# Splitting the first load by partitions and moving W2 from the end to the start of a decode kernel

## The chip, the core and the metric

The kernel runs on one core of one Trainium2 chip. The metric is device time in microseconds (us), the median of several executions. The engines are TensorE (PE in the profile, with its weight loads as PEld), VectorE (DVE), ScalarE (ACT), GpSimd (POOL) and SyncE (SP). SyncE does no arithmetic here: it issues the large loads. The data is moved by sixteen DMA engines.

## What is computed

One decode step of attention over a long cache, beside a small dense branch, mixed by a gate. Two sequences (B = 2), one token each, model width 448, 16 query heads and 8 key/value heads of width 256, and 32,768 cached positions.

```python
g = sigmoid((x * gate_w).sum(-1, keepdims=True))
# first branch (A): attention over the cache
q = (x @ wq).reshape(B, 1, 16, 256)            # wq: 448 x 4096
p = softmax(q @ k_cache.T * 256 ** -0.5)       # each K/V head serves two query heads
a = (p @ v_cache).reshape(B, 1, 4096) @ wo     # wo: 4096 x 448
# second branch (B): dense, GELU, dense
b = gelu(x @ w1 + b1) @ w2 + b2                # w1: 448 x 1792, w2: 1792 x 448
out = g * a + (1 - g) * b
```

The K and V caches are 2 x 8 x 32,768 x 256 bf16 values each, 268 MB each. They are nearly all of the bytes that are read.

## The kernel before: the parts that matter here

The caches come in as tiles of 128 partitions x 64 KB (8 MB). There are 32 K tiles and 32 V tiles. They rotate through a ring of three slots. SyncE walks through a fixed order of loads, and before each load it waits until PE is done with what lay in the slot.

```python
WOP = (0, 16, 28, 31, 32)          # WO is loaded and used in four pieces of these chunks
DQ = Dm // 2                       # 224: the output row is made in two column tiles
...
order = [("WQ", 0), ("W1", 0)]
for i in range(NTILES + LAG):      # K tiles, and V tiles two behind
    ...
order += [("V", LASTV), ("W2", 0), ("WO", 0)]
...
def released(d):                   # what PE must have done before a slot is filled again
    return {"K": ("S", idx, NCK // 2 - 1), "V": ("PV", idx), "WQ": "QT", "W1": "HT"}[kind]
```

The issue of the loads, on SyncE (cut to the kinds that matter):

```python
if kind == "WQ":      # 384 rows as 128 partitions x 24,576 B, and the 64 rows that are left
    parts = [(wq_f, A_wq[0:KC * P, :].rearrange("(p k) n -> p (k n)", p=P), "d_wq0"),
             (wq_r, A_wq[KC * P:Dm, :].rearrange("p (h n) -> (p h) n", h=2), "d_wq1")]
    for i, (o, src, _) in enumerate(parts):
        dma(lambda e, o=o, src=src: e.dma_start(o, src), "slot0", ("wq", i))
...
elif kind == "W2":
    dma(lambda e: e.dma_start(w2_f, B_w2.rearrange("(p f) n -> p (f n)", p=P)), "d_w2", "w2")
elif kind == "WO":
    for i in range(len(WOP) - 1):
        ...
```

The order on PE: the query projection (QT), the gate (GG), the first dense layer (HT) and the bias of the second (B2); then the loop over tiles (S: scores of a K tile; PV: probabilities times a V tile; OT: the sum of a group); and at the end the transposed attention vector (TT), the second dense layer (FB) and the output projection (FIN).

```python
do_QT(); do_GG(); do_HT(); do_B2()
...                                   # the loop over tiles
PV(LASTV - 1); PV(LASTV)
E.wait("pool", "ts1")
OT(NG - 1)
TT()
do_FB()
E.wait("dve", "at")
for i in range(len(WOP) - 1):
    FIN(i)
...
def do_FB():                          # line 459
    E.wait("dve", "hT")
    E.wait_total("d_w2")
    for fc in range(FC):              # 14 chunks
        for q in range(2):            # two column tiles of 224
            E.ins(lambda e, fc=fc, q=q: e.matmul(
                ps_a[64 * q:64 * q + Bn, :], hT_bf[:, fc, :], w2_v[:, fc, q * DQ:(q + 1) * DQ], ...))

def FIN(i):                           # line 551
    E.wait(f"pW{i}", ("wo", i))
    for c in range(WOP[i], WOP[i + 1]):
        for q in range(2):
            E.ins(lambda e, c=c, q=q: e.matmul(
                ps_a[64 * q:64 * q + Bn, :], attnT[:, c:Bn * NC:NC],
                wo_v[:, c * Dm + q * DQ:c * Dm + (q + 1) * DQ], ...))
```

When FIN is done, VectorE copies the first 224 columns of the output and ScalarE the others, and SyncE stores the row. Each copy raises one shared semaphore ("mix"), on which SyncE waits once.

Of the kernel before, what the change touches and what calls it, by code (L numbers as in the profile page):

```python
# [125 lines left out]
def bass_gated_mix__gqa_block_cached__dense_activation_gelu__decode_kernel(  # L126
# [26 lines left out]
    Bn, Sq, Dm = A_x.shape  # L153
    _, Hkv, Sk, Dh = A_k_cache.shape
    HD = A_wq.shape[1]
    Hq = HD // Dh
    Fd = B_w1.shape[1]
    assert Sq == 1 and Dh == 256 and Hq == 2 * Hkv and Bn == 2
    P = 128
    R = 128  # L160
    CR = 16
    NCK = R // CR
# [8 lines left out]
    KC = 3  # L171
    KR = Dm - KC * P
    assert 2 * KR == P
    HW, HF = HD // 2, Fd // 2
    FC = Fd // P
    SLOT = R * Dh
# [3 lines left out]
    assert (NTILES - LAG) % UNIT == 0  # L180
    PIECES = (64, 32, 32)
    NC = HD // P
    WOP = (0, 16, 28, 31, 32)
    DQ = Dm // 2
    GELU_C = 0.7978845608028654
    GELU_A = 0.044715

    sch = _Sched()
    for nm in ("pe", "act", "dve", "pool", "sp"):
        sch.stream(nm, 1)  # L190
    sch.stream("mix", 1)
    for i in range(NB):
        sch.stream(f"slot{i}", 16)
    for i in range(len(PIECES)):
        sch.stream(f"pV{i}", 16)
    for i in range(len(WOP) - 1):
        sch.stream(f"pW{i}", 16)
    for nm in ("d_w1", "d_w2", "d_x", "d_gw", "d_b", "d_out"):
        sch.stream(nm, 16)

    with contextlib.ExitStack() as es:
# [14 lines left out]
        b2_f = gp_sb  # L216
# [6 lines left out]
        dg = sb("dg", [Bn, Bn], dt.float32)  # L223
# [6 lines left out]
        hT_bf = sb("hT_bf", [P, FC, Bn], dt.bfloat16)  # L230
# [4 lines left out]
        out_sb = pexp[0:Bn, 0:Dm]  # L235
# [33 lines left out]
            b, kvh = grp(g)  # L269
            return cache[b, kvh, t * P * R:(t + 1) * P * R, :].rearrange("(p r) d -> p (r d)", p=P)  # L270

        W_WQ, W_W1 = KC * HD + HW, KC * Fd + HF
        assert W_WQ + W_W1 <= SLOT and (NC + FC) * Dm <= SLOT
        LASTV = NTILES - 1
        order = [("WQ", 0), ("W1", 0)]
        for i in range(NTILES + LAG):
            if i < NTILES:
                order.append(("K", i))
            if i >= LAG and i - LAG < LASTV:
                order.append(("V", i - LAG))  # L280
        order += [("V", LASTV), ("W2", 0), ("WO", 0)]
        slot_of = {("WQ", 0): 0, ("W1", 0): 0}
        rot = [d for d in order if d[0] in "KV" and d != ("V", LASTV)]
        for n, d in enumerate(rot):
            slot_of[d] = (n + 1) % NB
        s_wo = slot_of[("V", LASTV - 2)]
        slot_of[("WO", 0)] = slot_of[("W2", 0)] = s_wo
        slot_of[("V", LASTV)] = slot_of[("K", NTILES - 1)]
        assert len({s_wo, slot_of[("V", LASTV)], slot_of[("V", LASTV - 1)]}) == NB
        before_of, fill_no, occ, uses = {}, {}, {}, [0] * NB  # L290
        for d in order:
            s = slot_of[d]
            if d in (("W1", 0), ("WO", 0)):
                before_of[d] = []
                occ[s] = occ[s] + [d]
                continue
            before_of[d] = occ.get(s, [])
            occ[s] = [d]
            if d[0] in "KV" and d != ("V", LASTV):
                uses[s] += 1  # L300
                fill_no[d] = uses[s]

        def released(d):
            kind, idx = d
            return {"K": ("S", idx, NCK // 2 - 1), "V": ("PV", idx), "WQ": "QT", "W1": "HT"}[kind]

        cut = lambda s, lo, n: ring[:, s * SLOT + lo:s * SLOT + lo + n]
        wq_f, wq_r = cut(0, 0, KC * HD), cut(0, KC * HD, HW)
        wq_v = wq_f.rearrange("p (k n) -> p k n", k=KC)
        w1_f, w1_r = cut(0, W_WQ, KC * Fd), cut(0, W_WQ + KC * Fd, HF)  # L310
        w1_v = w1_f.rearrange("p (k n) -> p k n", k=KC)
        w2_f = cut(s_wo, NC * Dm, FC * Dm)
        w2_v = w2_f.rearrange("p (f n) -> p f n", f=FC)
        wo_v = cut(s_wo, 0, NC * Dm)

# [43 lines left out]
        def prog_sp(E):  # L359
            def dma(fn, stream, key):  # L360
                E.ins(fn, key=key, stream=stream)

            for d in order:
                for pd in before_of[d]:
                    E.wait("pe", released(pd))
                kind, idx = d
                if kind == "WQ":
                    parts = [(wq_f, A_wq[0:KC * P, :].rearrange("(p k) n -> p (k n)", p=P), "d_wq0"),
                             (wq_r, A_wq[KC * P:Dm, :].rearrange("p (h n) -> (p h) n", h=2), "d_wq1")]
                    for i, (o, src, _) in enumerate(parts):  # L370
                        dma(lambda e, o=o, src=src: e.dma_start(o, src), "slot0", ("wq", i))
                elif kind == "W1":
                    parts = [(w1_f, B_w1[0:KC * P, :].rearrange("(p k) n -> p (k n)", p=P)),
                             (w1_r, B_w1[KC * P:Dm, :].rearrange("p (h n) -> (p h) n", h=2))]
                    for i, (o, src) in enumerate(parts):
                        dma(lambda e, o=o, src=src: e.dma_start(o, src), "d_w1", ("w1", i))  # L376
                elif kind == "W2":
                    dma(lambda e: e.dma_start(w2_f, B_w2.rearrange("(p f) n -> p (f n)", p=P)), "d_w2", "w2")
                elif kind == "WO":
                    src = A_wo.rearrange("(p c) n -> p (c n)", p=P)  # L380
                    for i in range(len(WOP) - 1):
                        c0, c1 = WOP[i] * Dm, WOP[i + 1] * Dm
                        dma(lambda e, src=src, c0=c0, c1=c1: e.dma_start(wo_v[:, c0:c1], src[:, c0:c1]), f"pW{i}", ("wo", i))
                elif d == ("V", LASTV):
                    src, base, r0 = kv_src(A_v_cache, idx), slot_of[d] * SLOT, 0
                    for i, n in enumerate(PIECES):
                        c0, c1 = r0 * Dh, (r0 + n) * Dh
                        dma(lambda e, c0=c0, c1=c1: e.dma_start(ring[:, base + c0:base + c1], src[:, c0:c1]),
                            f"pV{i}", ("piece", i))
                        r0 += n  # L390
                else:
                    src = kv_src(A_k_cache if kind == "K" else A_v_cache, idx)
                    dma(lambda e, src=src, d=d: e.dma_start(cut(slot_of[d], 0, SLOT), src),
                        f"slot{slot_of[d]}", ("fill", d))
            E.wait_total("mix")
            dma(lambda e: e.dma_start(out[:, 0, :], out_sb), "d_out", "out")
            E.wait_total("d_out")

        def prog_pe(E):
# [4 lines left out]
            def do_QT():  # L404
# [3 lines left out]
                    E.ins(lambda e, k=k, src=src: e.matmul(ps_x[:, k, :], src, ident_b[0:Bn, 0:Bn],  # L408
                                                           start=True, stop=True), key=("XT" if k == KC + 1 else None))
                E.wait("act", "xT")  # L410
                E.wait("slot0", ("wq", 1))
                for h in range(Hq):
                    kvh, hh = h // 2, h % 2
                    for j in range(2):
# [17 lines left out]
                            key=("QR" if (s == NS - 1 and Q == 3) else None))  # L432

            def do_HT():
                E.wait_total("d_w1")
                E.wait("dve", "omB")
                for fc in range(FC):
                    for kc in range(KC):
                        E.ins(lambda e, fc=fc, kc=kc: e.matmul(
                            ps_hT[:, fc, :], w1_v[:, kc, fc:Fd:FC], xT[:, kc, :],  # L440
                            start=(fc == 0 and kc == 0), stop=False, skip_group_check=True))
                    for hf in range(2):
                        E.ins(lambda e, fc=fc, hf=hf: e.matmul(
                            ps_hT[hf * 64:hf * 64 + 64, fc, :], w1_r[:, fc:HF:FC], xT[:, KC + hf, :],
                            start=False, stop=True, skip_group_check=True),
                            key=("HT" if (fc == FC - 1 and hf == 1) else None))

            def do_B2():
                E.wait("dve", "b2f")
                for q in range(2):  # L450
                    E.ins(lambda e, q=q: e.matmul(ps_a[64 * q:64 * q + Bn, :], dg[:, :], b2_f[:, q * DQ:(q + 1) * DQ],
                                                  start=False, stop=False, skip_group_check=True))

            def do_FB():
                E.wait("dve", "hT")
                E.wait_total("d_w2")
                for fc in range(FC):
                    for q in range(2):
                        E.ins(lambda e, fc=fc, q=q: e.matmul(
                            ps_a[64 * q:64 * q + Bn, :], hT_bf[:, fc, :], w2_v[:, fc, q * DQ:(q + 1) * DQ],  # L460
                            start=False, stop=False, skip_group_check=True))

            def do_GG():
                E.wait("pool", "A0")
# [82 lines left out]
            def FIN(i):  # L547
                E.wait(f"pW{i}", ("wo", i))
                for c in range(WOP[i], WOP[i + 1]):
                    for q in range(2):  # L550
                        E.ins(lambda e, c=c, q=q: e.matmul(  # L551
                            ps_a[64 * q:64 * q + Bn, :], attnT[:, c:Bn * NC:NC],
                            wo_v[:, c * Dm + q * DQ:c * Dm + (q + 1) * DQ], start=False, stop=(c == NC - 1),
                            skip_group_check=True), key=("FIN" if (c == NC - 1 and q == 1) else None))

            def TT():
                E.wait("dve", "on")
                for b in range(Bn):
                    for dh in range(8):
# [6 lines left out]
            do_QT()  # L566
            do_GG()
            do_HT()
            do_B2()
            def K(idx):  # L570
                S(idx)
                if idx % NT == NT - 1:
# [14 lines left out]
            E.loop((NTILES - LAG) // UNIT, steps, ("dve", ("PT", 0)))  # L587
            PV(LASTV - 1)
            PV(LASTV)
            E.wait("pool", "ts1")  # L590
            OT(NG - 1)
            TT()
            do_FB()
            E.wait("dve", "at")
            for i in range(len(WOP) - 1):
                FIN(i)
# [1 line left out]
        def prog_act(E):  # L598
# [54 lines left out]
            E.loop(NG - 2, step, ("dve", ("PT", 0)))  # L653
            chain(NG - 1)
            E.wait("pe", "FIN")
            E.ins(lambda e: e.copy(out_sb[:, DQ:Dm], ps_a[64:64 + Bn, :]), key="mixa", stream="mix")

        def prog_dve(E):
            E.ins(lambda e: e.memset(ps_o[:, :], 0.0), key="o0")
# [130 lines left out]
            E.wait("pe", "TT")  # L790
            E.ins(lambda e: e.tensor_copy(attnT[:, :], ps_aT), key="at")
            E.wait("pe", "FIN")
            E.ins(lambda e: e.tensor_copy(out_sb[:, 0:DQ], ps_a[0:Bn, :]), key="mixd", stream="mix")

        progs = {"pool": prog_pool, "sp": prog_sp, "pe": prog_pe, "act": prog_act, "dve": prog_dve}
        engs = {nm: _Eng(sch, nm) for nm in progs}
# [45 lines left out]
```

## Time and profile before

| | |
|---|---|
| device time, median of 3 | 1273.89 us (1273.33 to 1274.27) |
| span of the profiled execution | 1271.6 us |
| mean granted TensorE clock | 0.783 |
| first load issued | 0.74 us after the span's start |
| first transpose of K0 on VectorE | 36.44 us |
| last WO matmuls (line 551) | 1267.90 to 1269.60 us |
| store of the output issued | 1270.05 us |

The profile is one execution of the program. It has the busy time of each engine, a digit per fortieth of the span for how busy each was, the DMA queues, the chain of work that ended last, groups of equal instructions, and the issues of transfers with the time until they landed. A line such as `L551` is a line of the kernel. In the timeline, a row gives the start, the length, the engine, the line, the operation, what is written and read, the count, and in brackets how long the engine stood idle before it and what ended that. The trace also holds the record of every DMA packet and the completion event of each of the sixteen DMA engines for each transfer.

### The profile page before, as it was taken

The numbers are of one execution on the slowest core, as the hardware profiler recorded it, in microseconds if no ns is written. First come the engines' busy times: TensorE is split into PE (matmuls) and PEld (weight loads), VectorE is DVE, ScalarE is ACT, GpSimd is POOL, SyncE is SP. The second block draws the span as 40 slices with busy tenths as digits, with TensorE's granted clock in tenths as the row PEclk, the third lists the DMA queues.
The fourth block names the chain that finished last, engine by engine and source line by source line (L and its number), as shares of the span: only waits on it lengthen the run. The fifth ranks groups of instructions, "written<-read, shape, count | busy, mean of one in ns | idle before, by whom it ended". The sixth has DMA issues, their size and how long they took to land.

```text
span 1271.6 us, 8088 instructions
## 1 busy us (share of the span) xinstructions
PE 698.9 (55%) x4544; PEld 146.0 (11%) x2016; DVE 685.8 (54%) x528; ACT 43.7 (3%) x183; POOL 3.3 (0%) x14
## 2 busy tenths in 40 slices
PE   4566566644466443665544665455664437655465
PEld 3111011100011100111100111000110001111012
DVE  2875537655365563556735466453755636566341
ACT  1000000000000000000000000000000000000000
POOL 1000000000000000000000000000000000000000
PEclk9988788767887777887778887778876778877686
DMA  9999999999999999999999999999999999999998
GB/s 404 441 434 431 429 429 435 431 439 434 431 429 435 437 431 437 435 431 429 433 439 431 437 435 429 431 433 439 431 437 433 431 431 433 439 431 433 437 423 359
DMA packets 10971, 547.59 MB, mean 431 GB/s; under 512 B 1352, under 2 KB 1616, under 8 KB 1872
## 3 DMA queue, kind: packets, MB, share of 16 engines
q1 hardware_dynamic: 10804, 547.43, 99.6%
q8 instruction: 8, 0.13, 0.0%
q10 hardware_dynamic: 156, 0.01, 0.0%
q14 instruction: 3, 0.02, 0.0%
HBM read 547.43 MB, written 0.00 MB: 431 GB/s over the span
## 4 chain that ended last, share of the span: by engine, by line
DMA 63%; DVE 21%; PE 13%; issue 3%; SPq 0%; another core or an unknown queue 0%
DMA ring<-in_A_k_cache_dram 60%; DVE ring L722 19%; PE ps_o L335 4%; PE ps_s L490 3%; PE ps_s L335 3%; DMA ring<-in_A_wo_dram 3%; DVE mx L726 1%; PE ps_o L539 1%; PE ps_m L499 0%; PE ps_m L504 0%; DVE gmax L728 0%; DVE gmx L732 0%; PE ps_f L551 0%; SPq L376 0%
## 5 line engine op out<-in xcount | busy, mean ns | idle before, releaser
L722 DVE STREAM_TRANSPOSE ring<-ring 128x2048 uint32<-128x2048 uint32 x256 | 565.2, 2275 | 390.2 <-DMA ring<-in_A_k_cache_dram 389.9
L490 PE MATMUL ps_s<-ring,Abd 128*128 128x512 bf16 x1024 | 427.0, 417 | 428.7 <-DVE ring L722 428.3
L335 PE MATMUL ps_s<-ring,Abd 128*128 128x512 bf16 x1024 | 423.3, 413 | 0.0
L490 PEld LDWEIGHTS ps_s<-ring,Abd 128*128 128x128 bf16 x1024 | 106.1, 104 | 852.0 <-DVE ring L722 480.1
L335 PE MATMUL ps_o<-ring,PT 128*24 128x512 bf16 x1504 | 112.9, 408 | 0.0
L539 PE MATMUL ps_o<-ring,PT 128*24 128x512 bf16 x544 | 58.1, 427 | 12.6 <-DMA ring<-in_A_v_cache_dram 12.6
L509 PE MATMUL ps_f<-o_sb,selg 128*32 128x257 f32 x32 | 17.0, 634 | 83.5 <-DVE o_sb L763 83.5
L763 DVE SCALAR_TENSOR_TENSOR o_sb<-ps_o,mask,o_sb 128x256 f32<-128x256 f32 x112 | 54.1, 483 | 8.9 <-PE ps_o L539 5.0
L726 DVE TENSOR_REDUCE mx<-ps_s 128x1 f32<-128x1024 f32 x16 | 19.6, 1224 | 59.9 <-PE ps_s L335 59.9
L636 ACT ACTIVATE negm<-ps_m 128x1 f32<-128x1 f32 x16 | 2.7, 171 | 1156.4 <-PE ps_m L504 1156.4
L739 DVE STREAM_TRANSPOSE PT<-pexp 128x1024 bf16<-128x1024 bf16 x16 | 19.9, 1245 | 36.8 <-PE ps_o L335 36.8
L539 PEld LDWEIGHTS ps_o<-ring,PT 128*24 128x24 bf16 x544 | 14.7, 100 | 104.1 <-issue 86.9
L736 DVE COPY ls<-lsum 128x1 f32<-128x1 f32 x16 | 2.5, 154 | 31.8 <-ACT pexp L640 31.8
L630 ACT COPY Abd<-qrep 32x16 bf16 (+1 forms) x128 | 19.4, 199 | 0.6
L640 ACT ACTIVATE pexp<-ps_s,negm 128x1024 bf16<-128x1024 f32 x16 | 17.8, 1113 | 1.7
L499 PE MATMUL ps_m<-ident_f,mx 128*1 128x128 f32 x32 | 6.1, 271 | 21.1 <-DVE mx L726 21.1
L760 DVE TENSOR_SCALAR o_sb<-ps_o,mask 128x256 f32<-128x256 f32 x16 | 7.6, 475 | 17.7 <-PE ps_o L335 17.7
L509 PEld LDWEIGHTS ps_f<-o_sb,selg 128*32 128x32 f32 x32 | 2.9, 139 | 101.6 <-DVE o_sb L763 99.5
L504 PE MATMUL ps_m<-ones_f,gmx 1*128 1x1 f32 x32 | 6.0, 256 | 9.9 <-DVE gmx L732 9.9
L728 DVE TENSOR_REDUCE gmax<-ps_m 1x2 f32<-1x128 f32 x16 | 4.5, 279 | 7.5 <-PE ps_m L499 7.5
L420 PE MATMUL ps_s<-xT,ring 128*128 128x2 bf16 x128 | 3.6, 165 | 8.1 <-DMA ring<-in_A_wq_dram 8.1
L504 PEld LDWEIGHTS ps_m<-ones_f,gmx 1*128 1x128 f32 x32 | 4.7, 183 | 14.6 <-DVE gmx L732 14.6
(76 smaller groups left out, 64.1 us busy)
## 6 DMA issues: line engine op xcount, KB each, us to landing
ring<-in_A_v_cache_dram SPq DMA_DIRECT2D x1, 4096.0 KB, 27.0
ring<-in_A_v_cache_dram SPq DMA_DIRECT2D x2, 2048.0 KB, 33.7
ring<-in_A_wq_dram SPq DMA_DIRECT2D x1, 3072.0 KB, 10.5
ring<-in_A_wo_dram SPq DMA_DIRECT2D x1, 1792.0 KB, 38.2
ring<-in_B_w_dram SPq DMA_DIRECT2D x1, 1568.0 KB, 34.3
ring<-in_B_w_dram SPq DMA_DIRECT2D x1, 1344.0 KB, 13.6
ring<-in_A_wo_dram SPq DMA_DIRECT2D x1, 1344.0 KB, 41.0
ring<-in_A_wq_dram SPq DMA_DIRECT2D x1, 512.0 KB, 11.3
```

Source lines behind the costliest of these rows:

```text
L335: return e.add_instruction(mybir.InstMatmult(name=f"I-{nc.next_id()}", engine=mybir.EngineType.PE, ldweights=False, ins=[e.lower_ap(x), e. ...
L490: fn = lambda e, o=o, x=x, st=st, sp=sp, s=s, w=w: e.matmul(o, a_win(s, w), x, start=st, stop=sp, skip_group_check=True)
L504: E.ins(lambda e: e.matmul(ps_m[:, C_BC:C_BC + 1], gmx[:, :], ones_f[0:1, 0:1], start=True, stop=True), key=("M2", g))
L509: E.ins(lambda e: e.matmul(ps_oa, selg[:, :], o_sb[:, :], start=False, stop=False, skip_group_check=True), key=("OT", g))
L539: fn = lambda e, o=o, x=x, wt=wt, st=st, sp=sp, j=j: e.matmul(o, wt, x, start=st, stop=sp, skip_group_check=True)
L630: E.ins(lambda e, o=o, Q=Q, c=c: e.copy(o[:, :, c:c + 2], qrep[32 * Q:32 * Q + 32, :, bass.ds(E.dyn(2 * g, 2), 2)]), key=(("A", g) if (Q = ...
L640: E.ins(lambda e: e.activation(pexp[:, :].rearrange("p (r i a) -> p i r a", r=CR, i=2), ps_s[:, :].rearrange("p (i r a) -> p i r a", i=2, ...
L722: E.ins(lambda e: e.transpose(k_words(idx, blk), k_words(idx, blk)), key=("T", idx, blk))
L726: E.ins(lambda e: e.tensor_reduce(mx[:, :], ps_s[:, :], AX.X, ALU.max), key=("MX", g))
L739: E.ins(lambda e: e.transpose(PT[:, :], pexp[:, :]), key=("PT", g))
L760: E.ins(lambda e, p=p, m=m: e.tensor_scalar(o_sb[:, 0:Dh], p, m, None, op0=ALU.mult), key=("OS0", g))
L763: E.ins(lambda e, p=p, m=m: e.scalar_tensor_tensor(out=o_sb[:, 0:Dh], in0=p, scalar=m, in1=o_sb[:, 0:Dh], op0=ALU.mult, op1=ALU.add), key= ...
```

## The change

Three things change together. The first load, the 128 partitions of wq, is issued as two transfers: partitions 0 to 15, and then partitions 16 to 127. W2 is loaded right behind W1 at the start, in the same slot, and the second dense layer (FB) is done there, so that the end of the kernel has only the attention output and WO left. The output row is made in four column tiles of 112 columns in place of two of 224, so that each engine copies two of them at the end. The pieces of WO have 14, 12, 4 and 2 chunks, in place of 16, 12, 3 and 1. The purpose is to take work and a transfer from the end of the kernel, and to let the first load begin in a small step.

```diff
-    WOP = (0, 16, 28, 31, 32)
-    DQ = Dm // 2
+    WOP = (0, 14, 26, 30, 32)
+    DQ = Dm // 4
...
-        order = [("WQ", 0), ("W1", 0)]
+        order = [("WQ", 0), ("W12", 0)]
...
-        order += [("V", LASTV), ("W2", 0), ("WO", 0)]
+        order += [("V", LASTV), ("WO", 0)]
...
-            return {"K": ("S", idx, NCK // 2 - 1), "V": ("PV", idx), "WQ": "QT", "W1": "HT"}[kind]
+            return {"K": ("S", idx, NCK // 2 - 1), "V": ("PV", idx), "WQ": "QT", "W12": "FB"}[kind]
...
-                    parts = [(wq_f, A_wq[0:KC * P, :].rearrange("(p k) n -> p (k n)", p=P), "d_wq0"),
-                             (wq_r, A_wq[KC * P:Dm, :].rearrange("p (h n) -> (p h) n", h=2), "d_wq1")]
+                    src = A_wq[0:KC * P, :].rearrange("(p k) n -> p (k n)", p=P)
+                    parts = [(wq_f[0:16, :], src[0:16, :]), (wq_f[16:P, :], src[16:P, :]),
+                             (wq_r, A_wq[KC * P:Dm, :].rearrange("p (h n) -> (p h) n", h=2))]
...
-                elif kind == "W1":
+                elif kind == "W12":
                     parts = [(w1_f, B_w1[0:KC * P, :].rearrange("(p k) n -> p (k n)", p=P)),
-                             (w1_r, B_w1[KC * P:Dm, :].rearrange("p (h n) -> (p h) n", h=2))]
+                             (w1_r, B_w1[KC * P:Dm, :].rearrange("p (h n) -> (p h) n", h=2)),
+                             (w2_f, B_w2.rearrange("(p f) n -> p (f n)", p=P))]
...
-            E.wait_total("mix")
+            E.wait("dve", "mix")
+            E.wait("act", "mix")
...
             def do_HT():
-                E.wait_total("d_w1")
+                E.wait_total("d_w12")
...
-            def do_B2():
+            def do_FB():
                 E.wait("dve", "b2f")
-                for q in range(2):
+                for q in range(4):
...
-            def do_FB():
                 E.wait("dve", "hT")
-                E.wait_total("d_w2")
                 for fc in range(FC):
-                    for q in range(2):
+                    for q in range(4):
...
             do_HT()
-            do_B2()
+            do_FB()
...
             OT(NG - 1)
             TT()
-            do_FB()
             E.wait("dve", "at")
...
-            E.ins(lambda e: e.copy(out_sb[:, DQ:Dm], ps_a[64:64 + Bn, :]), key="mixa", stream="mix")
+            for q in (2, 3):
+                E.ins(lambda e, q=q: e.copy(out_sb[:, q * DQ:(q + 1) * DQ], ps_a[32 * q:32 * q + Bn, :]),
+                      key=("mix" if q == 3 else None))
...
-            E.ins(lambda e: e.tensor_copy(out_sb[:, 0:DQ], ps_a[0:Bn, :]), key="mixd", stream="mix")
+            for q in (0, 1):
+                E.ins(lambda e, q=q: e.tensor_copy(out_sb[:, q * DQ:(q + 1) * DQ], ps_a[32 * q:32 * q + Bn, :]),
+                      key=("mix" if q == 1 else None))
```

More of the change, by code (lines that the diff above doesn't have):

```diff
@@ L190, in bass_gated_mix__gqa_block_cached__dense_activation_gelu__decode_kernel @@
         sch.stream(nm, 1)
-    sch.stream("mix", 1)
     for i in range(NB):
@@ L197, in bass_gated_mix__gqa_block_cached__dense_activation_gelu__decode_kernel @@
         sch.stream(f"pW{i}", 16)
-    for nm in ("d_w1", "d_w2", "d_x", "d_gw", "d_b", "d_out"):
+    for nm in ("d_w12", "d_x", "d_gw", "d_b", "d_out"):
         sch.stream(nm, 16)
@@ L270, in kv_src @@
             return cache[b, kvh, t * P * R:(t + 1) * P * R, :].rearrange("(p r) d -> p (r d)", p=P)
-        W_WQ, W_W1 = KC * HD + HW, KC * Fd + HF
-        assert W_WQ + W_W1 <= SLOT and (NC + FC) * Dm <= SLOT
+        W_WQ, W_W12 = KC * HD + HW, KC * Fd + HF + FC * Dm
+        assert W_WQ + W_W12 <= SLOT
         LASTV = NTILES - 1
-        order = [("WQ", 0), ("W1", 0)]
+        order = [("WQ", 0), ("W12", 0)]
         for i in range(NTILES + LAG):
@@ L280, in bass_gated_mix__gqa_block_cached__dense_activation_gelu__decode_kernel @@
                 order.append(("V", i - LAG))
-        order += [("V", LASTV), ("W2", 0), ("WO", 0)]
-        slot_of = {("WQ", 0): 0, ("W1", 0): 0}
+        order += [("V", LASTV), ("WO", 0)]
+        slot_of = {("WQ", 0): 0, ("W12", 0): 0}
         rot = [d for d in order if d[0] in "KV" and d != ("V", LASTV)]
@@ L286, in bass_gated_mix__gqa_block_cached__dense_activation_gelu__decode_kernel @@
         s_wo = slot_of[("V", LASTV - 2)]
-        slot_of[("WO", 0)] = slot_of[("W2", 0)] = s_wo
+        slot_of[("WO", 0)] = s_wo
         slot_of[("V", LASTV)] = slot_of[("K", NTILES - 1)]
@@ L292, in bass_gated_mix__gqa_block_cached__dense_activation_gelu__decode_kernel @@
             s = slot_of[d]
-            if d in (("W1", 0), ("WO", 0)):
+            if d == ("W12", 0):
                 before_of[d] = []
@@ L311, in bass_gated_mix__gqa_block_cached__dense_activation_gelu__decode_kernel @@
         w1_v = w1_f.rearrange("p (k n) -> p k n", k=KC)
-        w2_f = cut(s_wo, NC * Dm, FC * Dm)
+        w2_f = cut(0, W_WQ + KC * Fd + HF, FC * Dm)
         w2_v = w2_f.rearrange("p (f n) -> p f n", f=FC)
@@ L367, in prog_sp @@
                 if kind == "WQ":
-                    parts = [(wq_f, A_wq[0:KC * P, :].rearrange("(p k) n -> p (k n)", p=P), "d_wq0"),
-                             (wq_r, A_wq[KC * P:Dm, :].rearrange("p (h n) -> (p h) n", h=2), "d_wq1")]
-                    for i, (o, src, _) in enumerate(parts):
+                    src = A_wq[0:KC * P, :].rearrange("(p k) n -> p (k n)", p=P)
+                    parts = [(wq_f[0:16, :], src[0:16, :]), (wq_f[16:P, :], src[16:P, :]),
+                             (wq_r, A_wq[KC * P:Dm, :].rearrange("p (h n) -> (p h) n", h=2))]
+                    for i, (o, src) in enumerate(parts):
                         dma(lambda e, o=o, src=src: e.dma_start(o, src), "slot0", ("wq", i))
-                elif kind == "W1":
+                elif kind == "W12":
                     parts = [(w1_f, B_w1[0:KC * P, :].rearrange("(p k) n -> p (k n)", p=P)),
-                             (w1_r, B_w1[KC * P:Dm, :].rearrange("p (h n) -> (p h) n", h=2))]
+                             (w1_r, B_w1[KC * P:Dm, :].rearrange("p (h n) -> (p h) n", h=2)),
+                             (w2_f, B_w2.rearrange("(p f) n -> p (f n)", p=P))]
                     for i, (o, src) in enumerate(parts):
-                        dma(lambda e, o=o, src=src: e.dma_start(o, src), "d_w1", ("w1", i))
-                elif kind == "W2":
-                    dma(lambda e: e.dma_start(w2_f, B_w2.rearrange("(p f) n -> p (f n)", p=P)), "d_w2", "w2")
+                        dma(lambda e, o=o, src=src: e.dma_start(o, src), "d_w12", ("w12", i))
                 elif kind == "WO":
@@ L410, in do_QT @@
                 E.wait("act", "xT")
-                E.wait("slot0", ("wq", 1))
+                E.wait("slot0", ("wq", 2))
                 for h in range(Hq):
@@ L446, in do_HT @@
                             key=("HT" if (fc == FC - 1 and hf == 1) else None))
-            def do_B2():
+            def do_FB():
                 E.wait("dve", "b2f")
-                for q in range(2):
-                    E.ins(lambda e, q=q: e.matmul(ps_a[64 * q:64 * q + Bn, :], dg[:, :], b2_f[:, q * DQ:(q + 1) * DQ],
+                for q in range(4):
+                    E.ins(lambda e, q=q: e.matmul(ps_a[32 * q:32 * q + Bn, :], dg[:, :], b2_f[:, q * DQ:(q + 1) * DQ],
                                                   start=False, stop=False, skip_group_check=True))
-            def do_FB():
                 E.wait("dve", "hT")
-                E.wait_total("d_w2")
                 for fc in range(FC):
-                    for q in range(2):
+                    for q in range(4):
                         E.ins(lambda e, fc=fc, q=q: e.matmul(
-                            ps_a[64 * q:64 * q + Bn, :], hT_bf[:, fc, :], w2_v[:, fc, q * DQ:(q + 1) * DQ],
-                            start=False, stop=False, skip_group_check=True))
+                            ps_a[32 * q:32 * q + Bn, :], hT_bf[:, fc, :], w2_v[:, fc, q * DQ:(q + 1) * DQ],
+                            start=False, stop=False, skip_group_check=True),
+                            key=("FB" if (fc == FC - 1 and q == 3) else None))
             def do_GG():
@@ L549, in FIN @@
                 for c in range(WOP[i], WOP[i + 1]):
-                    for q in range(2):
+                    for q in range(4):
                         E.ins(lambda e, c=c, q=q: e.matmul(
-                            ps_a[64 * q:64 * q + Bn, :], attnT[:, c:Bn * NC:NC],
+                            ps_a[32 * q:32 * q + Bn, :], attnT[:, c:Bn * NC:NC],
                             wo_v[:, c * Dm + q * DQ:c * Dm + (q + 1) * DQ], start=False, stop=(c == NC - 1),
-                            skip_group_check=True), key=("FIN" if (c == NC - 1 and q == 1) else None))
+                            skip_group_check=True), key=("FIN" if (c == NC - 1 and q == 3) else None))
             def TT():
+                E.wait("pool", "ts1")
                 E.wait("dve", "on")
@@ L589, in prog_pe @@
             PV(LASTV)
-            E.wait("pool", "ts1")
             OT(NG - 1)
             TT()
-            do_FB()
             E.wait("dve", "at")
```

## The prediction

> **What bounds the kernel now.** I read the page first for the shares, then the DMA part, then the stretches at both ends, then the waits of the issuing queue, and last the timeline of the final microseconds.
>
> ```profile
> PE 698.9 (55%) x4544; PEld 146.0 (11%) x2016; DVE 685.8 (54%) x528; ACT 43.7 (3%) x183; POOL 3.3 (0%) x14
> ...
> DMA  9999999999999999999999999999999999999998
> ...
> q1 hardware_dynamic: 10804, 547.43, 99.6%
> ...
> HBM read 547.43 MB, written 0.00 MB: 431 GB/s over the span
> ```
>
> No compute engine is busy for more than 55% of the span, while the packets of the load queue fill 99.6% of sixteen DMA engines' span. 99.6% of 1271.6 us is 1266.5 us, so about 5 us in all are not transfer. The chain of waits puts 63% on DMA and names DVE and PE for the rest, but that chain walks through whichever instruction triggered the next issue; the queue itself always holds work:
>
> ```profile
> SPq L393 <- PE ps_s L335: 999.1, 31, 34.9
> ```
>
> And from the list of issues, with the median time to landing:
>
> ```profile
> ring<-in_B_w_dram SPq DMA_DIRECT2D x1, 1568.0 KB, 34.3
> ```
>
> SyncE waits some 32 us for a slot (999.1 / 31), yet a transfer lands 34.3 us (W2 here) to 49.7 us (a K tile, in the same list) after its issue, while one 8 MB tile needs 8.39 MB / 433 GB/s = 19.4 us. So between one and two tiles are always queued, and slot release never empties the queue. What can move the time is therefore the number of bytes (unchanged), the rate, and the two ends. Busy time by stretch shows the ends (columns: stretch and length, busy PE, PEld, DVE, ACT, POOL with counts, granted clock, DMA share, GB/s):
>
> ```profile
> 2.00:4.00 2.00, 0.00 (x0) 0.00 (x0) 2.00 (x10) 0.80 (x1) 1.85 (x5) 1.00 0.65 246
> 4.00:8.00 4.00, 0.27 (x5) 0.21 (x5) 0.08 (x1) 0.65 (x2) 0.02 (x1) 1.00 0.98 418
> ...
> 100.00:1200.00 1100.00, 597.53 (x3748) 113.92 (x1452) 594.87 (x436) 34.85 (x154) 0.00 (x0) 0.77 1.00 433
> ```
>
> The loads start slowly until about 4 us and then run at the level of the middle. The last microseconds, from the timeline:
>
> ```profile
> 1262.09 2.78 PE L459 MATMUL ps_f<-ring,hT_bf 128*2 128x224 bf16 x28
> 1264.76 2.14 PE L551 MATMUL ps_f<-ring,attnT 128*2 128x224 bf16 x32
> 1267.90 1.70 PE L551 MATMUL ps_f<-ring,attnT 128*2 128x224 bf16 x32 [1.00 <-DMA ring<-in_A_wo_dram]
> 1269.64 0.34 ACT L656 CAST pexp<-ps_f 2x224 bf16<-2x224 f32 x1 [45.75 <-PE ps_f L551]
> 1269.64 0.38 DVE L793 CAST pexp<-ps_f 2x224 bf16<-2x224 f32 x1 [7.21 <-PE ps_f L551]
> 1270.05 0.33 SPq L396 DMA_DIRECT2D out_dram<-pexp  x1
> ```
>
> The completion events of the four WO pieces are at 1264.62, 1267.85, 1268.67 and 1268.97 us. The last matmul ends at 1269.60, 0.63 after the last landing: the second piece's 24 matmuls had not drained. Then 0.45 us go to copy and issue, and about 1.5 us to landing the output and closing.
>
> [...] packets follow each other on an engine evenly (24,576 B in 0.912 us, 27 GB/s, from the single packets' records). [...] 32 matmuls of 32 columns in four column tiles take 0.41 us in all (line 428, from 16.46 us).
>
> **The change, part by part.**
> *Bytes.* W2 (1568 KB, 1.6 MB) leaves the end and joins the head. It takes 1.61 MB / 433 GB/s = 3.7 us of queue time in either place. All K and V tiles land 3.7 us later, the last WO byte at the same time as before. Gain in itself: 0. Packets per engine are equal (8 for W2, 8 for each WO piece); the one extra transfer adds a completion packet of 9 ns.
>
> *Head compute.* The first branch's matmuls now wait for W2 too. W1's completion is at 16.32 us, so W2's is near 20.1 us instead of HT's start at 18.48. HT ran until 25.2 (6.7 us); it would end near 27, GELU 2.2 us later (25.33 to 27.49 now), then 4 + 56 matmuls of 112 columns, four at a time: 14 groups x 0.09 us at half clock, 1.3 us. That is about 31 us, or 34 with the late head below. The first scores need K0, which landed at 36.4 and comes at 40 or later now, and slot 0 is wanted by K2, whose turn in the queue comes at 55.8 + 3.7 us. Cost: 0.
>
> *The split of the first load.* The sixteen first packets start at 1.76 to 2.73 us and end at 3.31 to 4.41 us, mean 3.70. The earliest data therefore flowed from 3.31 - 0.91 = 2.40 us. [...] What the split may gain is an earlier start of the later engines: at most 2.73 - 1.76 = 1.0 us for the last, 0.3 us in the mean. [...]
>
> *The tail.* The V tail comes 3.7 us later: the attention vector, cast at 1262.20 to 1262.42 now, is ready at 1266.2. FB's 2.78 us are gone from there. WO pieces of 14, 12, 4, 2 chunks land, scaled from 1260.33 (end of W2 now, of V then) to 1268.97, at 1264.1, 1267.4, 1268.4 and 1269.0. Each chunk is four matmuls of 112 columns, side by side: 93 ns at half clock (a pair of 224 columns is 187 ns in FB and 95.5 ns at full clock), 47 at full. The clock rose only at 1265.7, after FB's unbroken work, so without FB I expect half. Piece one: 1266.25 + 14 x 0.093 = 1267.55; piece two until 1268.7, piece three until 1269.05, piece four until 1269.25, plus 0.2 of pipeline: 1269.4 instead of 1269.60. Gain 0.2 us. Given back: two casts of 112 columns per engine in place of one of 224. A one-column DVE copy takes 0.14 us, so the 0.38 us cast holds about 0.1 us that is paid again: +0.1 us, and a second wait on SyncE, under 0.05. Tail: -0.05, give or take 0.3.
>
> [...]
>
> **Rivals.** (1) The split helps: the short transfer fills all queues at once and the start of the last engine moves from 2.73 towards 1.8. For it: an odd cut like 16 is hard to explain otherwise, and first packets take 1.0 to 2.4 us in place of 0.9. Against it: most of these end together near 3.6 us however early they began, which looks like first data coming late rather than packets queued late. It makes 1273.2 to 1273.8.
> (2) The 112-partition piece is dealt out in stripes rather than blocks, [...] I give it one chance in twenty.
> (3) The late branch removed from the end shows in full, because FB stood between the attention vector and WO: then 2.8 us would be won. Against it: the last landing at 1268.97 sets the end, PE was idle 1.00 us before the last pieces, and V comes 3.7 us later for it. I give it nothing.
> (4) A later W2 makes slot 0 late and empties the queue. Against it: 20 us of slack, above.
>
> **How the numbers follow.** [...] 1273.9 + 2.6 = 1276.5. The low end is the helped head, 1272.8[...]. Two per cent is 25.5 us, which nothing above reaches but the worst of rival 2: within 2% 0.98, slower 0.015, faster 0.005.
>
> **What would show it.** In the changed profile: bytes 547.43 MB again; the GB/s of 2 to 8 us well under 246 and 418; the load of wq's 112 partitions landing 2 us or more later than 11.19 us; K0's first transpose at 36.44 + 3.7 + the head's loss, so about 42 to 44 us; the last WO matmul within 0.5 us of the last landing; no wait for W2 in the tail. I am wrong if the head's rate is as before, if the first transpose is at 40.1, or if a gap opens in the middle.

## The result

The changed kernel takes 1279.09 us (median of 4, 1278.34 to 1279.26), the kernel before 1273.61 us (median of 4). The ratio is 1.0041, with a 95% interval from 1.0024 to 1.0059: slower by 5.5 us, clear of noise and far inside 2%. The prediction said 1276.5 with a range from 1272.8 to 1281.5.

The page of the changed kernel, the same lines as before:

```profile
PE 700.7 (55%) x4640; PEld 146.1 (11%) x2112; DVE 685.9 (54%) x529; ACT 43.9 (3%) x184; POOL 3.3 (0%) x14
...
DMA  9999999999999999999999999999999999999998
...
q1 hardware_dynamic: 10820, 547.43, 99.7%
...
HBM read 547.43 MB, written 0.00 MB: 429 GB/s over the span
```

Bytes are the same and busy times nearly so (PE has 96 matmuls more, in 700.7 us in place of 698.9); the sixteen more packets are the completions of one more transfer (1218 packets of 4 B in place of 1202). The share of 99.7% shows no idle time, and that is the trap of this view: a packet that is held up counts as busy. From their third round of sixteen on, wq's packets of 24,576 B take 1.29 to 1.65 us in the median of a round, before 0.91 to 0.92. The loss is in the rate, and only at the start. Busy time by stretch, with GB/s at the end of each row:

```profile
2.00:4.00 2.00, 0.00 (x0) 0.00 (x0) 2.00 (x10) 1.06 (x1) 1.85 (x5) 1.00 0.16 25
4.00:8.00 4.00, 0.27 (x5) 0.21 (x5) 0.08 (x1) 0.39 (x2) 0.02 (x1) 1.00 0.97 197
8.00:16.00 8.00, 0.00 (x0) 0.00 (x0) 1.87 (x6) 0.20 (x1) 0.00 (x0) 1.00 1.00 261
...
100.00:1200.00 1100.00, 613.27 (x3791) 116.81 (x1472) 603.20 (x439) 34.90 (x154) 0.00 (x0) 0.77 1.00 433
```

The kernel before, from 8 to 16 us:

```profile
8.00:16.00 8.00, 3.39 (x128) 3.42 (x128) 2.25 (x7) 0.20 (x1) 0.00 (x0) 1.00 1.17 493
```

From 4 to 8 us it is 197 GB/s in place of 418, and 261 in place of 493 up to 16 us, with the DMA share at 1.00 all the same. (A packet counts whole in the stretch where it starts, so over a few microseconds these figures are coarse, and a share can exceed 1.) From 100 us on it is 433 again, as before. The issue of wq before, and then its two issues in the changed kernel, with the time to landing:

```profile
ring<-in_A_wq_dram SPq DMA_DIRECT2D x1, 3072.0 KB, 10.5
```

```profile
ring<-in_A_wq_dram SPq DMA_DIRECT2D x1, 2688.0 KB, 16.0
...
ring<-in_A_wq_dram SPq DMA_DIRECT2D x1, 384.0 KB, 5.5
```

The completion events put numbers on the whole way: wq's 384 rows are complete at 17.16 us in place of 11.19 (+5.97). Partitions 0 to 15 are complete at 6.24, so the other 112 take 10.9 us for 2.75 MB, 252 GB/s; at 433 GB/s they would need 6.4. K0's first transpose is at 46.41 in place of 36.44 us (+9.97, of which about 3.7 are W2's own bytes, 1.61 MB at 433 GB/s):

```profile
46.41 17.66 DVE L721 STREAM_TRANSPOSE ring<-ring 128x2048 uint32<-128x2048 uint32 x8 [10.34 <-DMA ring<-in_A_k_cache_dram]
```

The last WO landing is at 1274.64 in place of 1268.97 us (+5.67), the last instruction at 1277.25 in place of 1271.59 (+5.66). What is lost in the first 17 us is still missing at the end, to within 0.3 us.

The tail changed its shape but not its length. The chain of waits of the changed kernel from the last piece of V on (start, length, what; L537 multiplies probabilities and V, L507 sums the group, L790 casts the attention vector, L549 is the output projection):

```profile
1230.04 35.94 DMA ring<-in_A_v_cache_dram
...
1266.02 1.92 PE ps_o L537 x16
...
1269.03 1.08 PE ps_f L507 x2
...
1271.62 0.23 DVE attnT L790
...
1271.90 3.19 PE ps_f L549 x128
```

The 128 matmuls of the output projection now run unbroken for 3.2 us, at a granted clock of 0.50, and start only when the attention vector is there. V's last piece lands at 1265.98, 9.1 us before they end. The last piece of WO lands at 1274.64, and its first matmul starts at 1274.68, in the pace of the row: it reaches the piece just as that lands, so V's path and WO's end together, and neither sets the end alone. The rows after it:

```profile
1275.11 0.54 DVE L793 CAST pexp<-ps_f 2x112 bf16<-2x112 f32 x2 [3.27 <-PE ps_f L549]
```

```profile
1275.71 0.32 SPq L396 DMA_DIRECT2D out_dram<-pexp  x1
```

From the last landing to the issue of the store it is 1275.71 - 1274.64 = 1.07 us, before 1270.05 - 1268.97 = 1.08.

### The profile page after: what moved, and what is told of

The parts are those of the page before. It is cut to its first block, busy times and chain, and to the rows that moved or that the text cites. A ratio compares the mean times of both kernels' runs of the same rounds, so it can differ in the third digit from the quotient of the medians.

```text
span 1277.3 us, 8288 instructions
## 1 busy us (share of the span) xinstructions
PE 700.7 (55%) x4640; PEld 146.1 (11%) x2112; DVE 685.9 (54%) x529; ACT 43.9 (3%) x184; POOL 3.3 (0%) x14
## 3 DMA queue, kind: packets, MB, share of 16 engines
q1 hardware_dynamic: 10820, 547.43, 99.7%
## 4 chain that ended last, share of the span: by engine, by line
DMA 63%; DVE 18%; PE 16%; issue 3%; SPq 0%; another core or an unknown queue 0%; DVEq 0%
DMA ring<-in_A_k_cache_dram 60%; DVE ring L721 16%; PE ps_s L488 5%; PE ps_s L334 5%; PE ps_o L334 4%; DMA ring<-in_A_v_cache_dram 3%; PE ps_o L537 1%; DVE mx L725 1%; PE ps_m L502 0%; PE ps_m L497 0%; DVE gmax L727 0%; PE ps_f L549 0%; DVE gmx L731 0%; SPq L377 0%
## 5 line engine op out<-in xcount | busy, mean ns | idle before, releaser
L334 PE MATMUL ps_o<-ring,PT 128*24 128x512 bf16 x1504 | 115.8, 416 | 0.0
L537 PE MATMUL ps_o<-ring,PT 128*24 128x512 bf16 x544 | 58.4, 428 | 12.7 <-DMA ring<-in_A_v_cache_dram 12.7
L507 PE MATMUL ps_f<-o_sb,selg 128*32 128x257 f32 x32 | 17.0, 635 | 83.4 <-DVE o_sb L762 83.4
L537 PEld LDWEIGHTS ps_o<-ring,PT 128*24 128x24 bf16 x544 | 14.8, 100 | 106.3 <-issue 89.3
L507 PEld LDWEIGHTS ps_f<-o_sb,selg 128*32 128x32 f32 x32 | 2.9, 139 | 102.2 <-DVE o_sb L762 102.2
```

The costliest lines, as they stand in the source:

```text
L334: return e.add_instruction(mybir.InstMatmult(name=f"I-{nc.next_id()}", engine=mybir.EngineType.PE, ldweights=False, ins=[e.lower_ap(x), e. ...
L507: E.ins(lambda e: e.matmul(ps_oa, selg[:, :], o_sb[:, :], start=False, stop=False, skip_group_check=True), key=("OT", g))
L537: fn = lambda e, o=o, x=x, wt=wt, st=st, sp=sp, j=j: e.matmul(o, wt, x, start=st, stop=sp, skip_group_check=True)
```

## The experiments

The theory: a transfer that writes only some of the 128 partitions runs at a lower rate for as long as it lasts, and nothing gives the time back. In the prediction the cost of such a transfer was the author's estimate: every load that SyncE issues in the kernel before writes all 128 partitions, so its trace could not show it. The rivals: any split or any short first transfer costs; W2 at the start or the new tail costs; the loss is made where HBM is read; it is a fixed cost of the kernel's start. The times below stand beside runs of the kernel before on the same chip, whose medians were 1273.12 to 1273.30 us.

### One part undone, one part alone

`e1_whole`, from the changed kernel:

```diff
-                    parts = [(wq_f[0:16, :], src[0:16, :]), (wq_f[16:P, :], src[16:P, :]),
+                    parts = [(wq_f, src),
```

> The changed kernel with the first load of wq whole again; W2 at the start and the four column tiles stay. If the split alone costs [...]: 1273.3 to 1274.0 us, the time of before, first transpose at 40.1 us. If W2 at the start or the new tail costs a part: 1275 us or more.

Measured: 1274.02 us (13 runs), ratio to before 1.0007, interval 0.9998 to 1.0015. The first transpose is at 40.12 us, and wq is complete at 10.96 us. The interval includes 1, but all 13 runs lie over the median of before, 1273.15 us. The split is the loss but for 0.9 us, to which `e5_shift` comes back.

`e2_split_only`, from the kernel before:

```diff
-                    parts = [(wq_f, A_wq[0:KC * P, :].rearrange("(p k) n -> p (k n)", p=P), "d_wq0"),
+                    src = A_wq[0:KC * P, :].rearrange("(p k) n -> p (k n)", p=P)
+                    parts = [(wq_f[0:16, :], src[0:16, :]), (wq_f[16:P, :], src[16:P, :]),
```

> The kernel before with nothing changed but the split of wq into 16 and 112 partitions. If the split alone costs: 1279 us, the first transpose 6 us later than 36.44. If the loss needs W2 at the start as well: under 1276 us.

Measured: 1279.21 us, ratio 1.0048 (1.0032 to 1.0063), 6.1 us over before. The first row of the transposes:

```profile
42.49 17.66 DVE L723 STREAM_TRANSPOSE ring<-ring 128x2048 uint32<-128x2048 uint32 x8 [9.09 <-DMA ring<-in_A_k_cache_dram]
```

42.49 - 36.44 = 6.05 us, and wq is complete at 17.11 us, as in the changed kernel. The split alone makes the whole loss; W2's place and the tail are not needed for it.

### Another cut

`e3_halves`, from the changed kernel:

```diff
-                    parts = [(wq_f[0:16, :], src[0:16, :]), (wq_f[16:P, :], src[16:P, :]),
+                    parts = [(wq_f[0:64, :], src[0:64, :]), (wq_f[64:P, :], src[64:P, :]),
```

> The changed kernel with wq split into 64 and 64 partitions. [...] 3.1 MB take some 14.5 us in place of 7.3: 6 to 7 us lost, 1280 us, packets of 24,576 B at 1.8 us all through both pieces. Theory that it is the short first transfer or the odd share of 7 packets per engine: no loss, 1273.5 to 1275 us.

Measured: 1281.02 us, ratio 1.0062 (1.0046 to 1.0077), 7.9 us over before. By stretch:

```profile
4.00:8.00 4.00, 0.27 (x5) 0.21 (x5) 0.09 (x1) 0.59 (x2) 0.03 (x1) 1.00 0.96 197
8.00:16.00 8.00, 0.00 (x0) 0.00 (x0) 1.87 (x6) 0.20 (x1) 0.00 (x0) 1.00 0.96 200
```

About 200 GB/s through both halves, and the single packets take 1.9 us where they took 0.91: 16 x 24,576 B / 1.91 us = 206 GB/s. At that rate 3.15 MB need 15.3 us in place of 7.3, 8.0 us more, which is the whole loss. Half of the partitions at a time had somewhat less than half of the 433 GB/s; the 14.5 us of the expectation, twice the 7.3, were an estimate of the author's for that half. No short first transfer and no odd share is needed.

`e4_columns`, from the changed kernel:

```diff
-                    parts = [(wq_f[0:16, :], src[0:16, :]), (wq_f[16:P, :], src[16:P, :]),
+                    parts = [(wq_f[:, 0:1536], src[:, 0:1536]), (wq_f[:, 1536:], src[:, 1536:]),
```

> The changed kernel with wq split by columns: 128 partitions x 3,072 B and then 128 x 21,504 B, the same bytes per transfer as 16 and 112 partitions. [...] no loss, 1273.3 to 1274.3 us. Theory that a short first transfer or one transfer more costs: 1277 to 1279 us.

Measured: 1272.97 us (12 runs), ratio 0.9999 (0.9991 to 1.0008).

```profile
4.00:8.00 4.00, 0.27 (x5) 0.22 (x5) 1.36 (x4) 0.61 (x3) 0.03 (x1) 1.00 0.99 420
8.00:16.00 8.00, 2.55 (x96) 2.58 (x97) 0.98 (x5) 0.00 (x0) 0.00 (x0) 1.00 0.99 414
```

The same bytes per transfer, cut the other way, cost nothing. Nor do they win anything: the sixteen first packets start at 1.77 to 2.07 us, as against 1.78 to 2.03 us in `e1_whole`. This is the changed kernel without its loss. It can't be told from the kernel before, so no version here beats both kernels.

### The disputed costs by themselves

These four start from the kernel before, with wq whole. Behind wq comes one more transfer into free columns of slot 0; its data is used by nobody, though the query projection waits for it as well.

```diff
+                    x0 = W_WQ + W_W1
+                    dma(lambda e: e.dma_start(ring[0:P, x0:x0 + 10640], <wq's rows>[0:P, 0:10640]), ...)    # d128
+                    dma(lambda e: e.dma_start(ring[16:P, x0:x0 + 12160], <wq's rows>[16:P, 0:12160]), ...)  # d112
+                    dma(lambda e: e.dma_start(ring[16:P, x0:x0 + 12160], <K tile 0>[16:P, 0:12160]), ...)   # d112k
+                    dma(lambda e: e.dma_start(ring[0:16, x0:x0 + 12160], <wq's rows>[0:16, 0:12160]), ...)  # d16
```

> The kernel before with one more transfer behind wq, whose data nobody uses: 128 partitions x 21,280 B (2.72 MB). It is the control: by bytes alone 2.72 MB / 433 GB/s = 6.3 us, 1279.4 us, give or take 1 us for the end. All theories expect this.

> The same 2.72 MB as partitions 16 to 127 x 24,320 B, behind a whole load of wq. If a transfer of 112 partitions is slow in itself [...]: 7 packets per engine at 1.3 to 1.7 us in place of 0.9, some 4.5 us over the 128-partition control, 1284 us. If the slow second piece in the changed kernel was only the backlog of the 16-partition piece: within 1 us of the control.

> The same destination, partitions 16 to 127 x 24,320 B, but read from the K cache, whose rows lie 65,536 B apart in place of 24,576 B. If the loss is made where the data is written [...]: the same packets and time as with wq as the source, 1284 us. If it is made where the data is read [...]: another packet time, up to no loss, 1279.4 us.

> The kernel before with one more transfer behind wq that nobody uses: partitions 0 to 15 x 24,320 B (389 KB). By bytes alone 0.9 us, 1274.1 us. [...]

Measured: `d128` 1279.52 us, 6.4 over before, as its bytes say. `d112` 1284.22 us: 4.7 us more for the same bytes. `d112k` 1284.69 us (1283.77 to 1284.95, over the range of `d112`, 1283.78 to 1285.03). `d16` 1277.50 us, 4.4 over before, 3.5 more than its 0.9 us of bytes. The issues of the extra transfer in `d128`, `d112` and `d112k`, in this order:

```profile
ring<-in_A_wq_dram SPq DMA_DIRECT2D x1, 2660.0 KB, 17.0
```

```profile
ring<-in_A_wq_dram SPq DMA_DIRECT2D x1, 2660.0 KB, 22.2
```

```profile
ring<-in_A_k_cache_dram SPq DMA_DIRECT2D x1, 2660.0 KB, 22.7
```

A transfer of partitions 16 to 127 is slow in itself, without 16 partitions ahead of it, and equally so from rows 24,576 or 65,536 B apart. That speaks against the reading side. 2.72 MB in 6.3 + 4.7 = 11.0 us are 248 GB/s. Every one of its packets is slowed: the medians of its seven rounds of sixteen are 1.30, 1.62, 1.68, 1.44, 1.43, 1.60 and 1.72 us in `d112`, the quickest of all is 0.99, and an undisturbed packet of 24,320 B would need 0.90, by the 0.91 of 24,576 B.

`d16s8` and `d16s7` spread the sixteen rows of `d16`:

```diff
-ring[0:16, x0:x0 + 12160]
+ring[0:128:8, x0:x0 + 12160]      # d16s8
+ring[0:112:7, x0:x0 + 12160]      # d16s7
```

> The unused transfer of 16 rows x 24,320 B behind wq goes to every eighth partition (0, 8, to 120)[...]. If any transfer of 16 partitions is slow: 1277.5 us as with partitions 0 to 15.

> The same to every seventh partition (0, 7, to 105)[...]. If any transfer of 16 partitions is slow: 1277.5 us.

Measured: 1275.71 us (ratio 1.0021, 1.0012 to 1.0031) and 1275.15 us (1.0015, 1.0009 to 1.0022). Over before and the 0.9 us of bytes that is 1.5 us with every eighth partition and 1.0 with every seventh, where partitions 0 to 15 cost 3.5. The first transposes of `d16`, `d16s8` and `d16s7`, in this order, against 36.44 before:

```profile
40.43 17.67 DVE L724 STREAM_TRANSPOSE ring<-ring 128x2048 uint32<-128x2048 uint32 x8 [8.57 <-DMA ring<-in_A_k_cache_dram]
```

```profile
38.57 17.66 DVE L724 STREAM_TRANSPOSE ring<-ring 128x2048 uint32<-128x2048 uint32 x8 [9.25 <-DMA ring<-in_A_k_cache_dram]
```

```profile
38.41 17.66 DVE L724 STREAM_TRANSPOSE ring<-ring 128x2048 uint32<-128x2048 uint32 x8 [8.80 <-DMA ring<-in_A_k_cache_dram]
```

Same number of partitions, same bytes, same rows read; only where they are written differs. What a transfer of 16 partitions loses depends on where its partitions lie (3.5, 1.5 and 1.0 us). Neighbours against every eighth is clear (first transposes 1.86 us apart); every eighth against every seventh is not, since the two intervals overlap and the first transposes are 0.16 us apart. Nor does spreading the rows take the whole loss away: in `d16s7` all sixteen packets take 1.09 to 1.61 us in place of 0.90. Why neighbours cost more is not shown.

`e6_k0`, from the kernel before, makes the split larger and moves it behind the start:

```diff
+                    if d == ("K", 0):
+                        o = cut(slot_of[d], 0, SLOT)
+                        dma(lambda e: e.dma_start(o[0:16, :], src[0:16, :]), f"slot{slot_of[d]}", ("head", d))
+                        dma(lambda e: e.dma_start(o[16:P, :], src[16:P, :]), f"slot{slot_of[d]}", ("fill", d))
+                        continue
```

> The kernel before with wq whole, and the first K tile (8 MB) in its place loaded as partitions 0 to 15 and then 16 to 127. If the loss is a lower rate for as long as such a transfer lasts [...], it grows with the bytes of a row: 65,536 B against 24,320 B, so 2.7 times the 3.5 us (16 partitions) and 4.7 us (112 partitions) of the unused transfers, 22 us: 1295 us, packets of 65,536 B at 3.5 to 4.5 us in place of 2.42. If it is a fixed cost of such a transfer or of the kernel's start: 6 to 8 us, 1280 us, or none.

Measured: 1294.96 us, ratio 1.0172 (1.0155 to 1.0189), 21.7 us over before. By stretch, while the 112 partitions come:

```profile
36.00:40.00 4.00, 0.00 (x0) 0.00 (x0) 0.00 (x0) 0.00 (x0) 0.00 (x0) 1.00 0.96 262
40.00:44.00 4.00, 0.00 (x0) 0.00 (x0) 0.00 (x0) 0.00 (x0) 0.00 (x0) 1.00 1.09 262
```

The loss grows with the bytes: a row 2.7 times as long costs 21.7 us in place of 3.5 + 4.7 = 8.2, 2.6 times as much. The 262 is sixteen packets of 65,536 B that happen to start in each 4 us. By the completion events the 112 partitions take from 26.52 to 57.64 us, 7.34 MB at 236 GB/s, near the 252 of the changed kernel's second piece. The loss is neither a fixed cost nor one of the start.

### The 0.9 us of e1_whole

The last landing of the kernel with wq whole, at 1268.52 us, is earlier than the 1268.97 of before, and yet it ends later. Its last rows on VectorE and SyncE:

```profile
1269.00 0.54 DVE L793 CAST pexp<-ps_f 2x112 bf16<-2x112 f32 x2 [3.27 <-PE ps_f L549]
```

```profile
1269.93 0.34 SPq L396 DMA_DIRECT2D out_dram<-pexp  x1
```

The store is issued 0.39 us after the copies, where the changed kernel needs 0.06. From the end of the copies to the last instruction it takes 1272.40 - 1269.54 = 2.86 us, in `e4_columns` 1271.11 - 1269.49 = 1.62. The packet records show two 8,192 B packets of an instruction queue, at 1270.62 and 1270.82 us, around the store's own. `e5_shift`, from `e1_whole`, moves that by one transfer more, of the same bytes:

```diff
-                             (wq_r, A_wq[KC * P:Dm, :].rearrange("p (h n) -> (p h) n", h=2))]
+                             *[(wq_r[:, c:c + HW // 2], A_wq[KC * P:Dm, :].rearrange("p (h n) -> (p h) n", h=2)[:, c:c + HW // 2])
+                               for c in (0, HW // 2)]]
```

> The kernel with wq whole, W2 at the start and four column tiles, and the small rest of wq loaded in two transfers of 256 KB in place of one of 512 KB: same bytes, one transfer more. Theory that the 0.9 us which the kernel with wq whole loses at its very end (store issued 0.39 us after the copies in place of 0.06, and landing later, beside a packet of the instruction queue) come from an instruction fetch that falls there: one transfer more shifts the fetch, the store is issued within 0.1 us of the copies, 1272.9 to 1273.3 us. Theory that W2 at the start or the new tail costs 0.9 us, or that a small first transfer gained it: 1273.9 to 1274.2 us.

Measured: 1273.42 us (13 runs, 1272.90 to 1273.57, all below the 1273.85 to 1274.40 of `e1_whole`), ratio to before 0.9999 (0.9991 to 1.0007).

```profile
1269.05 0.54 DVE L794 CAST pexp<-ps_f 2x112 bf16<-2x112 f32 x2 [3.27 <-PE ps_f L550]
```

```profile
1269.66 0.34 SPq L397 DMA_DIRECT2D out_dram<-pexp  x1
```

The gap is 0.07 us, from the copies to the last instruction it is 1.62 us again, and one of the two packets is now at 1235.5 us. The two kernels ran on different chips: against before on the same chip it is +0.87 us for `e1_whole` and +0.15 for `e5_shift`. So some 0.7 of the 0.9 us go with one more transfer, and the W2 move and the tail, which are in both, are not to blame. The spans of the thirteen executions of `e5_shift` lie at 1271.1 to 1271.3 us (six) and at 1271.6 to 1271.7 (seven), those of `e1_whole` at 1272.0 to 1272.6; the rows shown are of the first group, and what the second loses is not shown. That an instruction fetch is the cause is not shown either. Both packets in `e1_whole` start after the store was issued, 0.69 and 0.89 us, and the kernel before also has two of them at its end, at 1271.44 and 1272.59 us, with its store issued 0.03 us after the copies.

## Why the prediction was right, and where it was off

**What bounds the kernel** held. Bytes and the rate of the middle are unchanged, no wait opened there, and the loss at the start reaches the end.

**W2 at no cost** held: `e4_columns` and `e5_shift`, with W2 at the start and the new tail, stand at 0.9999 of before. The head's compute was indeed hidden: the second dense layer ends near 37.6 us, later than the 34 of the prediction, because the head came later, and K0's first transpose is at 46.41. Without the loss, in `e4_columns`, it ends at 31.8, where the prediction had 31.

**The 16 partitions** cost 1.4 us at the start. Their completion events are at 5.79 to 6.24 us; at 433 GB/s for the rest, the 11.19 us of before put this step at 11.19 - 6.36 = 4.83 us, 1.4 less than 6.24. Behind a whole load of wq, in `d16`, the same partitions cost 3.5 us.

**The 112 partitions** are the larger part of the loss. Measured by itself the piece costs 4.7 us, every packet is slowed in every round, and it runs at about 250 GB/s; in the changed kernel it takes 10.9 us in place of 6.4, 4.6 more. The 1.4 and the 4.7 make 6.1, against 6.05 us at the first transpose of `e2_split_only`. The 2.6 us that the prediction adds to 1273.9 were the author's estimate, a mean over cases with a loss from the split and without one, and no trace of before showed what the split costs. They are less than half of the 6.05, which is why the first transpose, at 46.41 us, missed the 42 to 44 of the prediction. How the rows are dealt to engines, and why all of them are slowed, no run shows. That the range held the result was in part luck: its upper end, 1281.5, rested on no measured loss either.

**The tail** was right in size: -0.05 predicted, -0.01 measured to the store's issue. The matmuls end 0.42 us after the last landing (0.43 predicted), at half clock as expected (0.50 granted from 1263.08 us on), four of 112 columns in 93 ns as predicted. The 0.2 us put for the pipeline are in the trace of before: a matmul of line 459 takes 0.39 us from start to end, while a pair follows the last after 0.19. The prediction also had the row run unbroken from the attention vector and reach WO's last piece as it lands, and so it does: the first matmul at 1271.90 follows the cast's end at 1271.85, and the last piece is used 0.04 us after it lands. The copies cost 0.16 us more (0.54 against 0.38), where 0.1 had been put, and the store is issued 0.06 us after them in place of 0.03, with the second wait.

**The rivals.** The helped start fell: the earliest packet starts at 1.76 us in the changed kernel, as before, and no cut made it earlier. Whether the 112 rows are dealt out in stripes or in blocks is not shown; the packets of `d112` take 1.3 to 1.7 us in the median of a round. The gain of FB's 2.8 us did not show (the store is issued 1.07 us after the last landing, before 1.08), nor did the late slot 0 (433 GB/s in the middle, as before).

## What to carry to other kernels

In a kernel whose load queue never idles (99.6% here), cut a transfer along its columns and leave all 128 partitions in each part: the same 393 KB ahead of the rest cost nothing in columns and, with the rest, 6 us in partitions. The price of a cut by partitions is a rate, so it grows with the bytes (22 us for one 8 MB tile), and since the DMA share stays near 100% (0.97 and 1.00 in the changed kernel's stretches at 197 and 261 GB/s) it must be read from GB/s by stretch and from the single packet's time. Moving W2 within this queue, which is always full, moved no time by itself (`e4_columns`, 0.9999 of before); look at what its consumer then has to wait for at either end.

## What was not expected

A transfer of partitions 16 to 127, which leaves out only an eighth of the partitions, runs at 236 to 252 GB/s in place of 433, with every packet slowed, from two different sources and with rows of 24,320 and 65,536 B. And a kernel of 1273 us lost about 0.7 us at its very end, behind the last copies, and one transfer more near its start took that away; the cause stays open. Differences of that size between two versions say nothing of the edit itself until the last rows of both are laid side by side.
